# Mask transposition and mask-column copy one place later in a hand-ordered attention and feed-forward kernel

## The chip, the cores and the metric

The kernel runs on one core of one Trainium2 chip. The metric is the device time of one execution in microseconds. TensorE is called PE here (its weight loads PEld), VectorE DVE, ScalarE ACT, GpSimd POOL, and SyncE, which issues most transfers, SP.

## The reference

One transformer block in bf16 over 2048 tokens of width 640. The first half is linear attention with 32 heads of 20 features each: the feature map of queries and keys is a pair of softmaxes over a small per-head projection. The second half is a feed-forward layer of width 1728 with SiLU.

```python
qkv = x @ wqkv                                   # x is layernormed first
pq, pk = q @ w_phi, k @ w_phi                    # per head, 20 x 20
phi_q = concat(softmax(pq), softmax(-pq))        # 40 features per head
phi_k = concat(softmax(pk), softmax(-pk))
kv  = einsum("bhsf,bhsd->bhfd", phi_k, v)        # sum over all tokens
z   = einsum("bhsf->bhf", phi_k)
num = einsum("bhqf,bhfd->bhqd", phi_q, kv)
den = einsum("bhqf,bhf->bhq", phi_q, z) + 1e-6
h   = A_x + (num / den) @ wo
h2  = h + silu(layernorm(h) @ w1) @ w2
```

`kv` and `z` sum over all tokens, so no output of the attention can be formed before the last token's key features are there.

## The kernel before

**Tiling.** The 2048 tokens are 16 tiles of 128 (numbers 0 to 15), in four groups of four for the query side. Everything is held in SBUF; PSUM is one tile `mm` of eight banks of 512 f32.

**Order.** No scheduler decides the order. The string ORDER lists steps one after another, each a word such as `kn.7.d`: the function `op_kn` called with 7 and "d". Within each engine the instructions run in just the order in which the steps issue them; between engines they wait on semaphores where data demands it. A number behind @ names the PSUM banks. So a step's place in the list sets what it stands behind on every engine that it uses.

**Steps around the change.** For each key tile t:

- `kp.t`, `kq.t`: TensorE projects the normalised tokens by folded key weights (line 374); `ke.t`: ScalarE takes exp(+) and exp(-) into `Ek` (line 406).
- `kr.t`: VectorE sums each head's exponentials, `Sk` (a reduction of 1280 elements, line 414), and takes the reciprocal (line 417).
- `kn.t.how`: the key normalisation, `Ek` times the reciprocal. "p" gives all 64 head halves to POOL (1280 elements, line 425). "d" gives 16 of 64 to POOL (320 elements, line 425) and 48 to VectorE (960 elements, line 429); "b" halves it (640 each).
- `vp.t`, `vq.t`, `vc.t`: value projection and its copy out.
- `cc.t`: TensorE adds the K-V product of tile t into bank 7 of PSUM (32 small matmuls, line 438). It needs all of tile t's normalised `Ek`. The last of the sixteen is `cc.7`.

Then the sum is turned into the right operand of the query side, `KVBD`, a tile with, for each sign s, five row groups and three places of 22 columns each. `kc` copies the sum out by ScalarE (`KVT`, line 452) and transposes it in 32 x 32 blocks by VectorE (`KVF`, line 453); `km.0` and `km.1` multiply it by the mask `maskS` into columns 0 to 20 of each place (VectorE, line 456). Column 21 is the mask itself; it makes the denominator. The mask is made early by POOL as `maskR` (`mc`, lines 213 to 220). The step `mt` transposes `maskR` to `maskS` on VectorE (line 226, 480 elements) and copies one of its columns into column 21 of `KVBD` for both signs on POOL (line 230, two instructions of 15 elements).

`dp.t` (line 515) multiplies query features `EqT` by `KVBD`; `dw`, `dr`, `do` form the quotient (VectorE, and POOL at line 550), `td` transposes by a transfer, `op` applies `wo` (line 577), and the feed-forward half follows: `up` (line 656), `ua`, `yp` (line 702), `yh` (lines 666 and 715 take the odd 64 features).

Between the keys, the query projections `qp`, `qs`, `qr`, `qt` (line 468) with `qe` (ScalarE, line 490) are laid into TensorE's order as filling.

**The order before the change** around it: `... cc.8 kn.15.p cc.6 vp.7@4 vq.7 vc.7.a mt qp.0.2@6 cc.15 cc.14 kr.7 kn.7.d cc.7 qs.0.2 kc qp.3.0@0 qs.3.0 qr.3.0 close km.0 km.1 qe.0.2 dp.0@2 ...`. On VectorE `mt` thus stands ahead of tile 7's reduction, on POOL its two copies stand ahead of `kn.7.d`'s 320 elements.

Of the kernel before, what the change touches and what calls it, by code (L numbers as in the profile page):

```python
# [41 lines left out]
kn.5.b kq.14 kp.6@0 lo.0.2.s l2.8.10.s cc.5 kr.13 l1.3.s kn.4.p kn.10.p cc.3 cc.4 ke.14 kr.8 kn.8.p kr.14  # L42
cc.12 xd.7 cc.2 kq.6 ke.6 kr.6 kn.14.b kp.15@4 kq.15 ke.15 kr.15 qp.0.0@2 kp.7@0 kq.7 ke.7 kn.6.p qp.0.1@4
qs.0.1 qr.0.1 kn.13.d qt.0.1 qe.0.1 vp.14@0 vq.14 vc.14.a qs.0.0 qr.0.0 qt.0.0 qe.0.0 cc.10 cc.13 cc.8
kn.15.p cc.6 vp.7@4 vq.7 vc.7.a mt qp.0.2@6 cc.15 cc.14 kr.7 kn.7.d cc.7 qs.0.2 kc qp.3.0@0 qs.3.0 qr.3.0
close km.0 km.1 qe.0.2 dp.0@2 qt.3.0 qe.3.0 qp.2.0@6 qs.2.0 qr.2.0 qt.2.0 dw.0.p dr.0 dp.1@2 dw.1.p qp.1.0@0
qs.1.0 qr.1.0 do.0.0.p do.0.1.p dr.1 do.1.0.p qe.2.0 l2.0.2.s do.1.1.p qt.1.0 qe.1.0 qp.1.1@6 dp.3@2 qs.1.1
qr.1.1 td.0 td.1 dw.3.p dr.3 qt.1.1 do.3.1.p do.3.0.p qp.3.2@0 qp.1.2@1 dp.2@2 dw.2.p dr.2 do.2.1.p do.2.0.p
# [24 lines left out]
def kernel(  # L73
# [11 lines left out]
    nc = tc.nc  # L85

    P = nc.NUM_PARTITIONS
    T = 16
    D = 640
# [46 lines left out]
    wTk = first.tile([P, C, D], BF16, name="wTk")  # L136
# [116 lines left out]
        nc.sync.dma_start_transpose(wTq[:, :, c * P : (c + 1) * P], A_wqkv[c * P : (c + 1) * P, 0:D])  # L253

    def op_lt(c, q="s"):
        nc.sync.dma_start_transpose(wTk[:, :, c * P : (c + 1) * P], A_wqkv[c * P : (c + 1) * P, D : 2 * D])

    def op_lo(a, b, q="s"):
        dma(q, wo[:, a:b, :], A_wo[a * P : b * P].rearrange("(c p) n -> p c n", p=P))
# [509 lines left out]
```

## Time and profile before

| | |
|---|---|
| median of three runs | 236.86 us (236.83 to 236.92) |
| the profiled execution | 236.84 us |
| its span, first to last instruction | 235.0 us |
| PE busy | 230.1 us, 98% |
| DVE busy | 131.3 us, 56% |
| ACT busy | 114.2 us, 49% |
| POOL busy | 96.1 us, 41% |

The span is what the trace covers; the rest of the profiled execution's time lies around it. All places in the trace are microseconds from the span's start. A row of the timeline gives start, length, engine, line, operation, output<-input and shape, and in brackets the engine's idle time ahead of it with what ended it. Matmul ends are modelled and POOL's are rough. Neighbouring rows of one engine may overlap by some hundredths of a microsecond.

### The profile page before, as it was taken

The page shows a single profiled execution, that of the slowest core. Times are in us where ns is not written, and L with a number is a line of the kernel's source. Part 1 is how long each engine was busy: PE and PEld are TensorE (multiplying, and loading weights), DVE is VectorE, ACT ScalarE, POOL GpSimd, SP SyncE. Part 2 cuts the span into 40 slices and gives each one's busy share as a digit, 9 for nine tenths or more (in the row PEclk, how much of TensorE's full clock was granted, in tenths as well). Part 3 has the DMA queues.
Part 4 walks back from the last instruction along what each step waited for, and adds up shares of the span by engine and source line. Part 5 has one row for each costly group of instructions (what it writes and reads, how often), then busy time and mean ns, then how long its engine had stood idle before and what let it go on. Part 6 is the DMA issues. An engine that isn't in the chain of part 4 may idle for free.

```text
span 235.0 us, 6302 instructions
## 1 busy us (share of the span) xinstructions
PE 230.1 (98%) x2676; PEld 148.1 (63%) x2676; DVE 131.3 (56%) x250; ACT 114.2 (49%) x172; POOL 96.1 (41%) x188
## 2 busy tenths in 40 slices
PE   8999999999999999999999999999999999999995
PEld 3877777776644556876754654467666567567762
DVE  3999989979948899886985445030442001101132
ACT  3979798777748775843317152652010431330100
POOL 7477986997924462587166201326030000000000
PEclk9999999999999999999999999999999999999999
DMA  7977997970001585532815510211152010000012
GB/s 201 320 268 125 130 272 149 231 189 0 6 3 28 121 121 148 54 67 56 137 33 98 101 31 0 56 31 29 33 137 56 28 31 28 28 3 28 28 37 77
DMA packets 44844, 20.67 MB, mean 88 GB/s; under 512 B 34448, under 2 KB 44304, under 8 KB 44816
## 3 DMA queue, kind: packets, MB, share of 16 engines
q1 hardware_dynamic: 43728, 19.88, 38.4%
q10 hardware_dynamic: 1088, 0.39, 0.7%
q8 instruction: 21, 0.34, 0.6%
q14 instruction: 7, 0.06, 0.1%
HBM read 9.61 MB, written 2.62 MB: 52 GB/s over the span
## 4 chain that ended last, share of the span: by engine, by line
PE 70%; ACT 1%; DVE 0%; POOL 0%; issue 0%
PE mm L702 24%; PE mm L656 24%; PE mm L577 9%; PE mm L468 8%; PE mm L515 3%; PE mm L666 1%; PE mm L715 1%; ACT EqT L490 1%; DVE ob L732 0%; POOL Ek L425 0%; PE mm L438 0%
## 5 line engine op out<-in xcount | busy, mean ns | idle before, releaser
L702 PE MATMUL mm<-w,shT 128*128 128x320 bf16 (+2 forms) x416 | 59.0, 299 | 0.0
L656 PE MATMUL mm<-HnT,w 128*128 128x512 bf16 (+1 forms) x325 | 58.6, 337 | 0.0
L702 PEld LDWEIGHTS <-shT 128*128 128x128 bf16 x416 | 39.6, 98 | 17.7 <-issue 1.3
L678 ACT ACTIVATE shT<-mm 128x1024 bf16<-128x1024 f32 (+2 forms) x29 | 27.4, 962 | 47.6 <-PE mm L656 35.5
L656 PEld LDWEIGHTS <-w 128*128 128x128 bf16 x325 | 31.6, 98 | 23.6
L723 DVE TENSOR_TENSOR ob<-mm,X 128x640 bf16<-128x640 f32 x15 | 12.1, 818 | 60.0 <-PE mm L702 42.7
L374 PEld LDWEIGHTS <-XnT 128*128 128x128 bf16 x320 | 30.6, 98 | 12.0
L550 POOL TENSOR_TENSOR o<-u,rd 128x320 bf16<-128x320 f32 x25 | 18.7, 764 | 41.8 <-DVE rd L544 35.4
L425 POOL TENSOR_TENSOR Ek<-Ek,Sk 128x1280 bf16<-128x1280 bf16 (+2 forms) x16 | 33.6, 2118 | 4.5 <-DVE Sk L417 2.9
L594 ACT ACTIVATE sq<-X 128x640 bf16<-128x640 bf16 x16 | 11.7, 734 | 32.4 <-DVE X L586 29.5
L414 DVE TENSOR_REDUCE Sk<-Ek 128x64 f32<-128x1280 bf16 x16 | 23.3, 1455 | 2.6 <-ACT Ek L406 2.6
L374 PE MATMUL mm<-Wfk,XnT 128*128 128x320 bf16 x160 | 24.5, 299 | 0.0
L577 PE MATMUL mm<-wo,ot 128*128 128x320 bf16 x160 | 23.7, 300 | 0.3 <-ACT EqT L490 0.3
L468 PE MATMUL mm<-XnT,Wfq 128*128 128x512 bf16 x100 | 24.0, 380 | 0.0
L374 PE MATMUL mm<-wv,XnT 128*128 128x320 bf16 x160 | 23.5, 299 | 0.0
L490 ACT ACTIVATE EqT<-mm 128x1024 bf16<-128x1024 f32 (+1 forms) x24 | 19.7, 879 | 6.1 <-PE mm L468 6.0
L406 ACT ACTIVATE Ek<-mm 128x640 bf16<-128x640 f32 x32 | 20.6, 717 | 3.8 <-PE mm L374 1.8
L586 DVE SCALAR_TENSOR_TENSOR X<-mm,X 128x640 bf16<-128x640 f32 x16 | 12.9, 820 | 14.3 <-PE mm L577 14.0
L577 PEld LDWEIGHTS <-ot 128*128 128x128 bf16 x160 | 15.3, 98 | 6.9 <-issue 0.2
L468 PEld LDWEIGHTS <-Wfq 128*128 128x128 bf16 x100 | 9.1, 98 | 9.2
L536 DVE TENSOR_TENSOR u<-mm,w 128x672 f32<-128x672 f32 x16 | 13.7, 858 | 1.2 <-DVE w L534 0.2
L539 DVE TENSOR_TENSOR u<-u,mm 128x672 f32<-128x672 f32 x16 | 13.6, 853 | 0.6
(78 smaller groups left out, 204.9 us busy)
## 6 DMA issues: line engine op xcount, KB each, us to landing
out_dram<-ob SPq DMA_DIRECT2D x15, 160.0 KB, 1.8
w<-in_B_w_dram SPq DMA_DIRECT2D x6, 360.0 KB, 4.5
X<-in_A_x_dram SPq DMA_DIRECT2D x3, 640.0 KB, 6.6
w<-in_B_w_dram SPq DMA_DIRECT2D x5, 320.0 KB, 4.1
wk<-in_A_wqkv_dram SPq DMA_DIRECT2D x4, 160.0 KB, 4.2
wv<-in_A_wqkv_dram SPq DMA_DIRECT2D x1, 480.0 KB, 7.4
wo<-in_A_wo_dram SPq DMA_DIRECT2D x1, 480.0 KB, 5.9
w<-in_B_w_dram SPq DMA_DIRECT2D x1, 480.0 KB, 4.0
```

The costliest lines, as they stand in the source:

```text
L374: nc.tensor.matmul(ps[:, half, 0:320], tok(XnT[t // GT], t)[:, c, :], W[:, c, half * 320 : (half + 1) * 320], start=(c == 0), stop=(c == C ...
L406: nc.scalar.activation(Ek[:, s, :].rearrange("p (a n) -> p a n", a=2), tl["kp", t][:, :, 0:320], AF.Exp, scale=1.0 - 2.0 * s,)
L414: nc.vector.tensor_reduce(Sk[:], tl["ek", t][:].rearrange("p s (h f) -> p (s h) f", f=DH), axis=AX.X, op=ALU.add,)
L425: nc.gpsimd.tensor_tensor(Ek3[:, 0:n], Ek3[:, 0:n], Sk[:, 0:n].unsqueeze(2).to_broadcast([P, n, DH]), op=ALU.mult,)
L468: nc.tensor.matmul(tl["qp", g, i][:, k, :], Wfq[:, c, r * P : (r + 1) * P], XnT[g][:, c, :], start=(c == 0), stop=(c == C - 1),)
L490: nc.scalar.activation(E[:, s, rs[0] : rs[-1] + 1, :], tl["qp", g, i][:, 0 : len(rs), :], AF.Exp, scale=1.0 - 2.0 * s,)
L536: nc.vector.tensor_tensor(u[:], A[1][:, :, :, 0:21], w[:].unsqueeze(3).to_broadcast([P, 4, 8, 21]), op=ALU.mult,)
L550: (nc.vector if eng == "v" else nc.gpsimd).tensor_tensor(tl["o", t][:, a * 320 : (a + 1) * 320].rearrange("p (h f) -> p h f", f=DH), tl["u ...
L577: nc.tensor.matmul(ps[:, half, 0:320], tl["ot", t][:, c, :], wo[:, c, half * 320 : (half + 1) * 320], start=(c == 0), stop=(c == C - 1),)
L656: nc.tensor.matmul(ps[:, i * W : (i + 1) * W], w1[:, c, fc * P : (fc + 1) * P], HnT[g][:, c, 0:W], start=(c == 0), stop=(c == C - 1), skip ...
L678: nc.scalar.activation(sh[:, a:b], tl["up", g, k][:, 0 : b - a], AF.Silu)
L702: nc.tensor.matmul(ps, shT[g][:, fc * W + i * P : fc * W + (i + 1) * P], w2[:, fc, a:b], start=first and fc == 0, stop=last and fc == FC - ...
```

## The change

The word `mt` moves five words to the right in ORDER, from behind `vc.7.a` to behind `kn.7.d`. On VectorE that is past tile 7's reduction, reciprocal and multiplication; on POOL past tile 7's 320-element multiplication; the other words between issue nothing on these two engines. The second hunk lets the step `lt` choose a queue; no word `lt` stands in ORDER.

```diff
-kn.15.p cc.6 vp.7@4 vq.7 vc.7.a mt qp.0.2@6 cc.15 cc.14 kr.7 kn.7.d cc.7 qs.0.2 kc qp.3.0@0 qs.3.0 qr.3.0
+kn.15.p cc.6 vp.7@4 vq.7 vc.7.a qp.0.2@6 cc.15 cc.14 kr.7 kn.7.d mt cc.7 qs.0.2 kc qp.3.0@0 qs.3.0 qr.3.0
...
     def op_lt(c, q="s"):
-        nc.sync.dma_start_transpose(wTk[:, :, c * P : (c + 1) * P], A_wqkv[c * P : (c + 1) * P, D : 2 * D])
+        (nc.sync if q == "s" else nc.scalar).dma_start_transpose(wTk[:, :, c * P : (c + 1) * P], A_wqkv[c * P : (c + 1) * P, D : 2 * D])
```

## The prediction

> **What bounds the kernel now.** I read the first page of the profile first, then the chain of work that ended last in order of time, then the waits and the timeline of the stretch in which the change lies (58 to 74 us).
>
> ```profile
> span 235.0 us, 6302 instructions
> PE 230.1 (98%) x2676; PEld 148.1 (63%) x2676; DVE 131.3 (56%) x250; ACT 114.2 (49%) x172; POOL 96.1 (41%) x188
> PEclk9999999999999999999999999999999999999999
> ```
>
> TensorE (PE) is busy for 98% of the span at a full granted clock in every slice, so time can be won only where it stands still, and an engine off its path matters only where TensorE waits for it. The chain says where it did, from 65 us to the end:
>
> ```profile
> 65.26 0.65 POOL Ek L425
> 65.91 0.04 issue
> 65.95 0.37 PE mm L438 x32
> 66.33 2.27 PE mm L468 x10
> 68.59 0.40 PE mm L515 x38
> ...
> 86.91 0.02 issue
> 86.93 1.95 ACT EqT L490 x2
> 88.88 0.04 issue
> 88.92 1.52 PE mm L577 x10
> ...
> 232.29 0.29 DVE ob L732
> ```
>
> Columns are start, length, engine and line. The chain begins with one POOL instruction, the normalisation of token tile 7's keys (L425 in `kn.7.d`), on which TensorE's last K-V product (`cc.7`, L438) waits. After it the chain is TensorE's own work but for one stretch of ScalarE at 86.93, which itself followed matmuls. What starts `cc.7` earlier should thus move all that follows, to the end. How long TensorE stood there:
>
> ```profile
> PE mm L438 <- POOL Ek L425: 0.6, 1, 0.6
> ```
>
> ```profile
> 59.76 1.33 DVE L429 TENSOR_TENSOR Ek<-Ek,Sk 128x960 bf16<-128x960 bf16 x1
> 61.01 0.66 DVE L226 STREAM_TRANSPOSE maskS<-maskR 128x480 bf16<-128x480 bf16 x1
> 61.61 1.44 DVE L414 TENSOR_REDUCE Sk<-Ek 128x64 f32<-128x1280 bf16 x1
> 63.08 0.55 DVE L417 RECIPROCAL Sk<-Sk 128x64 f32<-128x64 f32 x1
> 63.74 1.27 DVE L429 TENSOR_TENSOR Ek<-Ek,Sk 128x960 bf16<-128x960 bf16 x1
> 63.94 1.32 POOL L230 COPY KVBD<-maskS 128x15 bf16<-128x15 bf16 x2
> 64.71 0.66 PE L438 MATMUL mm<-Ek,Vp 128*21 128x40 bf16 x64
> 65.18 0.72 POOL L425 TENSOR_TENSOR Ek<-Ek,Sk 128x320 bf16<-128x320 bf16 x1
> 65.95 0.37 PE L438 MATMUL mm<-Ek,Vp 128*21 128x40 bf16 x32 [0.58 <-POOL Ek L425]
> 66.44 0.42 ACT L452 CAST KVT<-mm 128x320 bf16<-128x320 f32 x1 [1.35 <-PE mm L438]
> 66.89 0.51 DVE L453 STREAM_TRANSPOSE KVF<-KVT 128x320 bf16<-128x320 bf16 x1 [1.89 <-ACT KVT L452]
> 67.44 0.57 DVE L456 TENSOR_TENSOR KVBD<-KVF,maskS 128x315 bf16<-128x315 bf16 x2
> 68.53 0.47 PE L515 MATMUL mm<-KVBD,EqT 32*128 32x44 bf16 x40
> 72.31 1.41 POOL L550 TENSOR_TENSOR o<-u,rd 128x320 bf16<-128x320 f32 x2 [6.41 <-PE mm L468]
> ```
>
> TensorE is through with `cc.15` and `cc.14` at 64.71 + 0.66 = 65.37 and starts `cc.7` at 65.95: 0.58 us of standing still. That is all there is to win here. Ahead of that wait lie, on POOL, the two mask copies (L230), and on VectorE (DVE) the mask transposition (L226). Both are moved behind tile 7's normalisation.
>
> **Part by part.** *VectorE.* The transposition leaves its place at 61.01, so tile 7's reduction starts 61.61 - 61.01 = 0.60 us earlier (its input is older: the reduction followed L226 without a wait), the reciprocal at 62.48, and the multiplication L429 is ready at 63.14 in place of 63.74. Whether that helps depends on POOL, whose single instructions in this stretch are:
>
> ```profile
> 57.36 2.71 POOL L425 TENSOR_TENSOR Ek<-Ek,Sk 128x1280 bf16<-128x1280 bf16 x1 [0.69 <-ACT Ek L406]
> ```
>
> ```profile
> 60.04 1.64 POOL L425 TENSOR_TENSOR Ek<-Ek,Sk 128x320 bf16<-128x320 bf16 x1
> ```
>
> ```profile
> 61.64 2.35 POOL L425 TENSOR_TENSOR Ek<-Ek,Sk 128x1280 bf16<-128x1280 bf16 x1
> ```
>
> ```profile
> 63.94 1.18 POOL L230 COPY KVBD<-maskS 128x15 bf16<-128x15 bf16 x1
> ```
>
> The same 320-element POOL instruction took 0.72 us at 65.18, with VectorE idle, and 1.64 us at 60.04, when L429 ran on VectorE until 59.76 + 1.33 = 61.09; it ended at 61.68, 0.59 us behind that. The first mask copy took 1.18 us (the second 0.25, below), and ended at 65.12, 0.11 us behind the other L429 (63.74 + 1.27 = 65.01). The other way round, both L429 of 960 elements ended exactly 1.02 us after the 1280-element POOL instruction in front of them: 61.09 against 57.36 + 2.71 = 60.07, and 65.01 against 61.64 + 2.35 = 63.99. So I read L429 on VectorE and the bf16 instructions on POOL as shutting each other out: who has begun, finishes, and the other waits.
>
> Then the 0.60 us on VectorE is worth nothing: L429, ready at 63.14, still waits for POOL's instruction of `kn.15` to end at 63.99, and ends at 63.99 + 1.02 = **65.01**, as before.
>
> *POOL.* With the copies gone from in front of it, the 320-element instruction of `kn.7` comes up at 63.94, finds VectorE waiting longer than itself, as at 60.04, and ends 0.59 us behind L429: 65.01 + 0.59 = **65.60**, against 65.18 + 0.72 = 65.90 before. Gain **0.30 us**. Its ends: if nothing of it were done during the wait, 65.01 + 0.72 = 65.73, gain 0.17; if the two engines did not shut each other out, all of TensorE's 0.58. I take 0.30, since the 60.04 row is the same instruction behind the same L429.
>
> The Trainium skill (SBUF — State Buffer, section "A bandwidth-pool intuition that's wrong (but worth ruling out)") says that a GpSimd operation behind a VectorE one on the shared port is blocked until the VectorE one ends plus about 115 ns. The copy's 0.11 us agrees. With a whole 0.72 behind it, the 320-element instruction would by that end at 65.01 + 0.115 + 0.72 = 65.85, an estimate from that page, and the gain would be 0.05; the 0.59 measured behind the earlier L429 speaks for the larger one.
>
> *TensorE* started `cc.7` 0.05 us behind POOL's end (65.90 to 65.95), so it starts at 65.65, and stands still for 0.28 us in place of 0.58.
>
> *The moved steps in their new place.* L226 (0.66) follows L429 at once and ends by 65.01 + 0.66 = 65.67. VectorE's next is L453, at 66.89 - 0.30 = 66.59 then: 0.9 us to spare. In its old place L226 ran its 0.66 beside a POOL instruction of the same kind, so I don't count it as shut out. The copies:
>
> ```profile
> L230 POOL COPY KVBD<-maskS x2: 247/713/1179, 63.9 to 65.0; 128x15 bf16<-128x15 bf16 x2
> ```
>
> Alone 0.25 us each, behind 65.67 they end at about 66.25. They are now due only where TensorE reads their column of `KVBD`, in `dp.0` (L515), which comes at 68.53 - 0.30 = 68.23: 2.0 us of cover, and VectorE's write of the same tile (L456, 67.14 then) comes 0.9 us behind them. POOL's next work is L550 at 72.31. So the move costs nothing as long as these two covers hold; without them every 0.1 us costs 0.1. Nothing is moved past a DMA; neither step issues one, and SP's order is unchanged. The changed `op_lt` is never called in ORDER: zero.
>
> *A wait more on TensorE.* In the built order L515's first weight load now waits for VectorE and its first matmul for POOL, once for each half of `KVBD`; before, only the matmul waited. Both semaphores are long up. Behind them stand all later matmuls. The nearest row is the one event instruction of that queue:
>
> ```profile
> L438 PEldq EVENT_SEMAPHORE  x1: 51/51/51, 65.2 to 65.2; - x1
> ```
>
> Between nothing and 2 x 0.05 = 0.10 us; it can't be less than nothing, since a wait starts nothing earlier. I take nothing: TensorE goes from L468 to L515 with loads ahead of matmuls, and a wait that is already met has only its issue to pay.
>
> **Sum.** The profiled execution took 236.84 us, 1.84 around its span of 235.0. 236.84 - 0.30 = 236.54; the median of the runs stands 0.02 above the profiled one, so **236.56 us**, 0.13% less. With the ends 0.17 and 0.41 (0.30 and the 0.11 by which the copy ended behind L429, if that handover were hidden too), and up to 0.10 for the waits, the forecast's own range is 236.45 to 236.75 (236.86 - 0.41, and 236.86 - 0.17 + 0.10 = 236.79, cut by a little).
>
> **The rivals.** *All of the stall goes.* If L429 can run at 63.14 beside POOL, it ends at 63.14 + 1.02 = 64.16 and POOL's 320 elements at 63.94 + 0.72 = 64.66, ahead of TensorE's 65.37. Then the 0.58 us go, and perhaps some of the overlap between one group of matmuls and the next: 64 matmuls took 0.66 and 32 took 0.37, so 32 add 0.29 and each group has 0.08 of run-out. 236.86 - 0.58 to - 0.66 gives 236.20 to 236.28. For it: the rows of POOL's instructions are only ends as recorded. Against it: twice the same 1.02 us from POOL's end to L429's, and two POOL instructions that end just behind L429's end. 0.20.
>
> *POOL goes first.* If POOL hands on from instruction to instruction, its 320 elements run at 63.94 to 64.66, and L429 from there to 65.68; `cc.7` starts at 65.73 and the gain is 0.22: 236.64, inside the forecast's range. Against it: at 60.04 and at 63.94 VectorE got in between. 0.07.
>
> *Slower: the mask column becomes the last input of `dp.0`.* The copies now share their moment with what VectorE does for `KVBD`. If they take the long row, 1.18 us each, from 65.67 to 68.03, the multiplication L456 (two inputs in SBUF like L429), ready at 67.14, is shut out until 68.03 and ends at 68.60; `dp.0` starts at 68.65 in place of 68.23, and 0.42 lost against 0.30 won makes 236.98. It decides from the moment that the copies end later than 68.23 - 0.05 - 0.57 = 67.61. Against it: the long row had L429 beside it, the short one didn't, and in the new place VectorE is idle but for L226. To lose over 0.2% the copies would have to end behind 68.38. 0.07.
>
> *Given back later* (a DMA or ScalarE result that TensorE meets 0.3 us sooner): 236.86. For it: the 86.93 row, where TensorE waits for ScalarE; against it: that one hangs on TensorE's own matmuls and moves with them. 0.06. *The change doesn't do what it says:* the built orders differ in just the moved rows. Nothing.
>
> **How the numbers follow.** Forecast 0.60, all of the stall 0.20, POOL first 0.07, given back 0.06, slower 0.07. The range reaches from the stall rival's lower end to the forecast's upper one, 236.2 to 236.75, and leaves about 0.13 out. 0.2% is 0.47 us, about what a measurement of this kernel can tell from no change; the forecast lies inside that. Below 236.39: the stall rival, 0.20, and a little of the forecast, 0.02. Above 237.33: 0.05 of the slower rival. Within: the rest, 0.73.
>
> **What would show it.** In the profile after: L429 of `kn.7` starting at 63.1 with a duration of about 1.87 us and ending near 65.0; POOL's 320-element instruction taking about 1.66 us from 63.94; TensorE's wait at L438 about 0.3 us; L226 at 65.0 and two short copies behind it; L515 at 68.2. L429 ending near 64.2 shows the stall rival; a copy over 1 us beside L456, or a wait of L515 on POOL, the slower one. A new wait of TensorE on a DMA would make the sum wrong.

## The result and the profile after

The changed kernel takes 236.45 us (median of 20 runs, 236.34 to 236.69) against 236.84 us of the kernel before (20 runs, 236.69 to 237.16): ratio 0.9984, 95% interval 0.9978 to 0.9991. That is 0.39 us less, with an interval of 0.21 to 0.52, against the 0.30 forecast. The change made the kernel a little faster, by less than the 0.2% that the prediction set as its bound.

The profiled execution took 236.37 us. From the first page of its profile:

```profile
span 234.7 us, 6283 instructions
PE 228.1 (97%) x2657; PEld 148.0 (63%) x2676; DVE 131.8 (56%) x250; ACT 114.2 (49%) x172; POOL 96.1 (41%) x188
```

PE counts 19 matmuls fewer only because their records are missing (PEld has all 2676). DVE is busy 0.5 us longer, though it runs the same instructions. Where that comes from is seen in the timeline of the stretch around the change (start, length, engine, line, operation):

```profile
59.70 1.33 DVE L429 TENSOR_TENSOR Ek<-Ek,Sk 128x960 bf16<-128x960 bf16 x1
60.95 1.47 DVE L414 TENSOR_REDUCE Sk<-Ek 128x64 f32<-128x1280 bf16 x1
62.46 0.55 DVE L417 RECIPROCAL Sk<-Sk 128x64 f32<-128x64 f32 x1
63.11 1.83 DVE L429 TENSOR_TENSOR Ek<-Ek,Sk 128x960 bf16<-128x960 bf16 x1
64.65 0.66 PE L438 MATMUL mm<-Ek,Vp 128*21 128x40 bf16 x64
64.86 0.67 DVE L226 STREAM_TRANSPOSE maskS<-maskR 128x480 bf16<-128x480 bf16 x1
65.58 0.37 PE L438 MATMUL mm<-Ek,Vp 128*21 128x40 bf16 x32 [0.27 <-POOL Ek L425]
65.60 0.40 POOL L230 COPY KVBD<-maskS 128x15 bf16<-128x15 bf16 x2
66.52 0.51 DVE L453 STREAM_TRANSPOSE KVF<-KVT 128x320 bf16<-128x320 bf16 x1 [0.98 <-ACT KVT L452]
68.15 0.47 PE L515 MATMUL mm<-KVBD,EqT 32*128 32x44 bf16 x40
71.94 1.41 POOL L550 TENSOR_TENSOR o<-u,rd 128x320 bf16<-128x320 f32 x2 [5.94 <-DVE rd L544]
```

And POOL's two instructions ahead of the copies, each from a narrow window of the same timeline:

```profile
61.58 2.35 POOL L425 TENSOR_TENSOR Ek<-Ek,Sk 128x1280 bf16<-128x1280 bf16 x1
```

```profile
63.89 1.64 POOL L425 TENSOR_TENSOR Ek<-Ek,Sk 128x320 bf16<-128x320 bf16 x1
```

Tile 7's multiplication on VectorE (L429) starts 0.63 us earlier than before (63.11 for 63.74) and lasts 0.56 us longer (1.83 for 1.27): nearly all that the departed transposition gave was spent waiting inside L429's own duration, until POOL's 1280 elements ended at 61.58 + 2.35 = 63.93. It ends at 64.94. POOL's 320 elements, up at 63.89, last 1.64 in place of 0.72 and end at 65.53, 0.59 behind L429. TensorE starts `cc.7` at 65.58, having stood still for 0.27 us in place of 0.58.

Since executions differ a little ahead of this stretch, I measure it from the start of the matmuls of `cc.15` and `cc.14` to the first product with `KVBD` (L515): before 68.53 - 64.71 = 3.82 us, now 68.15 - 64.65 = 3.50. That 0.32 us is the change's effect. The two profiled executions differ by more, by 236.84 - 236.37 = 0.47. Ahead of the stretch the changed kernel's trace is already 0.06 us earlier (64.65 for 64.71): its first load of X landed 0.09 us earlier, as the first VectorE row of each kernel shows, before and after:

```profile
3.89 0.49 DVE L274 BATCH_NORM_STATS2 stats<-X 128x6 f32<-128x320 bf16 x1 [3.89 <-DMA X<-in_A_x_dram]
```

```profile
3.80 0.49 DVE L274 BATCH_NORM_STATS2 stats<-X 128x6 f32<-128x320 bf16 x1 [3.80 <-DMA X<-in_A_x_dram]
```

From L515 on, the two traces run alike to the start of the last VectorE additions, before and after:

```profile
231.57 1.02 DVE L732 TENSOR_TENSOR ob<-mm,X 128x512 bf16<-128x512 f32 x2 [1.92 <-PE mm L702]
```

```profile
231.19 1.02 DVE L732 TENSOR_TENSOR ob<-mm,X 128x512 bf16<-128x512 f32 x2 [1.93 <-PE mm L702]
```

That is 231.57 - 68.53 = 163.04 before and 231.19 - 68.15 = 163.04 now: nothing was given back. The additions start 0.38 us earlier, which is 0.32 + 0.06; the other 0.09 of the 0.47 lies behind them and around the span, in time that the trace does not cover (1.84 us before, 1.67 now, from the rounded spans).

### The profile page after: what moved, and what is told of

It is laid out like the page before. It is cut to its first block, busy times and chain, and to the rows that moved or that the text cites. A ratio compares the mean times of both kernels' runs of the same rounds, so it can differ in the third digit from the quotient of the medians.

```text
span 234.7 us, 6283 instructions
## 1 busy us (share of the span) xinstructions
PE 228.1 (97%) x2657; PEld 148.0 (63%) x2676; DVE 131.8 (56%) x250; ACT 114.2 (49%) x172; POOL 96.1 (41%) x188
## 4 chain that ended last, share of the span: by engine, by line
PE 91%; POOL 2%; ACT 2%; DMA 1%; issue 1%; DVE 1%
PE mm L702 24%; PE mm L656 24%; PE mm L374 18%; PE mm L577 9%; PE mm L468 8%; PE mm L515 3%; POOL Ek L425 2%; PE mm L438 1%; DMA X<-in_A_x_dram 1%; PE mm L666 1%; PE mm L715 1%; PE mm L342 1%; ACT EqT L490 1%; ACT wTk L173 0%; PE mm L313 0%
## 5 line engine op out<-in xcount | busy, mean ns | idle before, releaser
L425 POOL TENSOR_TENSOR Ek<-Ek,Sk 128x1280 bf16<-128x1280 bf16 (+2 forms) x16 | 34.5, 2176 | 4.8 <-DVE Sk L417 3.7
L468 PE MATMUL mm<-XnT,Wfq 128*128 128x512 bf16 x90 | 22.1, 379 | 1.1 <-issue 1.0
```

The costliest lines, as they stand in the source:

```text
L425: nc.gpsimd.tensor_tensor(Ek3[:, 0:n], Ek3[:, 0:n], Sk[:, 0:n].unsqueeze(2).to_broadcast([P, n, DH]), op=ALU.mult,)
L468: nc.tensor.matmul(tl["qp", g, i][:, k, :], Wfq[:, c, r * P : (r + 1) * P], XnT[g][:, c, :], start=(c == 0), stop=(c == C - 1),)
```

## The experiments

**The theory:** VectorE's multiplication with two inputs in SBUF and POOL's bf16 instructions shut each other out, so on the path to `cc.7` lies the sum of POOL's `kn.15`, VectorE's `kn.7` and POOL's `kn.7`, plus whatever stands between them on POOL. Of the moved step only the two copies were part of that sum. **The first rival:** VectorE's 0.60 us earlier start brought the gain. **The second:** all instructions on tile 7's `Ek` are held in order for some other reason, with the memory of the inputs playing no part.

All medians and ratios below are against the kernel before on the same chip. "Stretch" is the one defined above, "wait" TensorE's at `cc.7`.

| kernel | stretch us | wait us | median us | before us | ratio (95% interval) |
|---|---|---|---|---|---|
| before | 3.82 | 0.58 | 236.84 | | |
| changed | 3.50 | 0.27 | 236.45 | 236.84 | 0.9984 (0.9978 to 0.9991) |
| changed_again | 3.51 | 0.28 | 236.55 | 236.96 | 0.9984 (0.9975 to 0.9992) |
| changed_third | 3.51 | 0.27 | 236.75 | 237.06 | 0.9985 (0.9976 to 0.9994) |
| copies_late | 3.50 | 0.27 | 236.62 | 236.97 | 0.9986 (0.9978 to 0.9995) |
| transpose_early | 3.81 | 0.59 | 236.98 | 236.97 | 1.0000 (0.9991 to 1.0009) |
| both_early | 3.50 | 0.27 | 236.72 | 236.97 | 0.9989 (0.9980 to 0.9998) |
| second_input_psum | 3.13 | none | 236.64 | 236.97 | 0.9984 (0.9975 to 0.9993) |
| second_input_psum_again | 3.14 | none | 236.63 | 236.96 | 0.9985 (0.9977 to 0.9994) |
| vector_all | 3.25 | none shown | 236.42 | 236.96 | 0.9981 (0.9972 to 0.9989) |
| vector_all_again | 3.26 | none shown | 236.39 | 237.06 | 0.9966 (0.9953 to 0.9979) |
| vector_all_psum | 3.12 | none | 236.26 | 237.06 | 0.9967 (0.9954 to 0.9979) |
| split_half | 3.71 | 0.48 | 236.93 | 236.96 | 1.0006 (0.9994 to 1.0018) |
| extra_idle | 3.51 | 0.27 | 236.90 | 237.06 | 0.9989 (0.9980 to 0.9998) |

A stretch is read from one trace; where the same kernel was traced again it came out within 0.01 us. A median here is of twenty runs in the first two rows and of eleven or twelve below (six and five for vector_all_psum and vector_all_again), and scatters by some 0.1 to 0.2 us. So the mechanism is read from the stretch and from the rows, the gain from the ratios.

### One half of the change alone

The step `mt` is cut in two: `mt` keeps the transposition, a new step `mu` makes the two copies.

```diff
 # copies_late, from the kernel before
+    def op_mu():
+        [nc.gpsimd.tensor_copy(KVBD[:, s, :, :, 21], maskS[:, :, :, 0]) for s in range(2)]
-kr.7 kn.7.d cc.7
+kr.7 kn.7.d mu cc.7
```

> Only the two mask copies move behind tile 7's key normalisation; the mask transposition stays ahead of tile 7's reduction, as in the kernel before. Theory (VectorE's two-input multiplication and POOL's bf16 instructions shut each other out, so only the copies were on the path): L429 of tile 7 is ready at 63.7, ends near 65.0, POOL's 320 elements end 0.59 behind it, TensorE waits about 0.28 us at the last K-V product, and the time is that of the changed kernel, 0.3 us (0.13%) under before. Rival (VectorE's 0.60 us earlier start brought the gain): the time is that of before, TensorE's wait 0.5 to 0.6 us.

```diff
 # transpose_early, from the kernel before, with op_mu
-ke.14 kr.8 kn.8.p kr.14
+ke.14 kr.8 mt kn.8.p kr.14
-vc.7.a mt qp.0.2@6
+vc.7.a mu qp.0.2@6
```

> The mask transposition moves into VectorE's idle stretch ahead of the reduction at 53.2 us; the two copies stay ahead of tile 7's 320 elements on POOL. So tile 7's reduction is 0.60 us earlier and the copies are still in the way. Theory: L429 of tile 7 starts at 63.1 but ends near 65.0 all the same, the first copy still takes over 1 us, TensorE's wait stays at 0.58 us and the time is that of before. Rival (VectorE's earlier start brought the gain): L429 ends near 64.2 to 64.4, TensorE's wait falls to 0.3 us or less, 0.3 us or more under before.

The two halves come out as far apart as they can. With only the copies moved, the stretch is the changed kernel's; the transposition still stands ahead of the reduction, and L429 starts as late as before, relative to its neighbours. The timeline of copies_late, and POOL's 320 elements from a narrow window:

```profile
61.11 0.67 DVE L226 STREAM_TRANSPOSE maskS<-maskR 128x480 bf16<-128x480 bf16 x1
63.83 1.27 DVE L429 TENSOR_TENSOR Ek<-Ek,Sk 128x960 bf16<-128x960 bf16 x1
65.64 0.40 POOL L230 COPY KVBD<-maskS 128x15 bf16<-128x15 bf16 x2
65.74 0.38 PE L438 MATMUL mm<-Ek,Vp 128*21 128x40 bf16 x32 [0.27 <-POOL Ek L425]
```

```profile
64.05 1.64 POOL L425 TENSOR_TENSOR Ek<-Ek,Sk 128x320 bf16<-128x320 bf16 x1
```

L429 ends at 63.83 + 1.27 = 65.10, and POOL's 320 elements end 0.59 us behind it, at 65.69, as in the changed kernel. With only the transposition out of the way, L429 starts early, lasts long, and nothing is won. The timeline of transpose_early:

```profile
61.21 1.47 DVE L414 TENSOR_REDUCE Sk<-Ek 128x64 f32<-128x1280 bf16 x1
63.37 1.83 DVE L429 TENSOR_TENSOR Ek<-Ek,Sk 128x960 bf16<-128x960 bf16 x1
64.14 1.32 POOL L230 COPY KVBD<-maskS 128x15 bf16<-128x15 bf16 x2
65.38 0.72 POOL L425 TENSOR_TENSOR Ek<-Ek,Sk 128x320 bf16<-128x320 bf16 x1
66.15 0.37 PE L438 MATMUL mm<-Ek,Vp 128*21 128x40 bf16 x32 [0.59 <-POOL Ek L425]
```

L429 ends at 63.37 + 1.83 = 65.20, the copies behind it, POOL's 320 elements at 66.10: the order of before, wait included. The first rival falls.

### The step's new place

```diff
 # both_early, from the kernel before, with op_mu
-ke.14 kr.8 kn.8.p kr.14
+ke.14 kr.8 mt kn.8.p kr.14
-ke.6 kr.6 kn.14.b
+ke.6 kr.6 mu kn.14.b
-vc.7.a mt qp.0.2@6
+vc.7.a qp.0.2@6
```

> The transposition in VectorE's idle stretch ahead of 53.2 us, and the copies in POOL's idle stretch at 54.7 us, both long before tile 7. Theory: as the changed kernel, TensorE's wait about 0.28 us, 0.3 us under before; where the step goes does not matter once the copies are away from tile 7. Rival (the new place behind tile 7's normalisation has a cost of its own, in the waits at the query product or in the copies beside VectorE's work on the same tile): up to 0.1 us faster than the changed kernel.

The stretch is again 3.50 us. In this kernel's order L515 waits for VectorE alone, as before the change. So neither the new wait of L515 on POOL nor the copies' nearness to L456 costs anything that the trace shows; the new place is free, and the earlier one, away from tile 7, does as well.

### What the shutting out hangs on

```diff
 # second_input_psum, from the changed kernel
-kr.7 kn.7.d mt
+ks.7@0 kt.7 mt
...
-        nc.vector.reciprocal(Sk[:], Sk[:])
+        tl["skp", t] = mm1()[:, 0:48]
+        nc.vector.reciprocal(tl["skp", t], Sk[:, 16:64])
+        nc.vector.reciprocal(Sk[:, 0:16], Sk[:, 0:16])
...
+            Ek3[:, 16:], Ek3[:, 16:], tl["skp", t].unsqueeze(2).to_broadcast([P, 48, DH]), op=ALU.mult,
```

The step `ks.7@0` puts 48 of the 64 reciprocals into PSUM bank 0, which is free then.

> The changed kernel, with tile 7's reciprocals of the 48 head halves that VectorE multiplies written to a free PSUM bank, so that L429's counterpart has one input in SBUF and one in PSUM; one small reciprocal more on VectorE for POOL's 16 halves. Theory (the shutting out comes from two SBUF inputs): VectorE's multiplication runs beside POOL's 1280 elements from about 63.2, for 1.0 to 1.1 us, ends near 64.3; POOL's 320 elements take 0.6 to 0.8 us from 63.9 and end near 64.6; TensorE does not wait at the last K-V product, and the time is 0.55 to 0.65 us under before. Rival (the two engines shut each other out for any reason bound to the shared tile Ek or to order): VectorE's multiplication ends near 65.0, and the time is that of the changed kernel.

The timeline, with L750 and L747 in the places of L429 and L425 of tile 7, and POOL's instruction ahead of them from a narrow window:

```profile
63.37 1.15 DVE L750 TENSOR_TENSOR Ek<-Ek,mm 128x960 bf16<-128x960 bf16 x1
64.23 0.72 POOL L747 TENSOR_TENSOR Ek<-Ek,Sk 128x320 bf16<-128x320 bf16 x1
64.97 0.94 PE L438 MATMUL mm<-Ek,Vp 128*21 128x40 bf16 x96
68.10 0.47 PE L515 MATMUL mm<-KVBD,EqT 32*128 32x44 bf16 x40
```

```profile
61.91 2.35 POOL L425 TENSOR_TENSOR Ek<-Ek,Sk 128x1280 bf16<-128x1280 bf16 x1
```

The same multiplication, writing the same tile at the same place, now runs from 63.37 to 64.52 straight through the last 0.89 us of POOL's 1280 elements (to 64.26), and POOL's 320 elements take 0.72 although 0.29 of that lies beside it. TensorE runs the 96 matmuls without a gap. What shut the two engines out was the second input in SBUF. The second rival falls. The Trainium skill (SBUF — State Buffer, section "Who interferes with whom") says that a VectorE instruction with two SBUF inputs contends with a GpSimd instruction that reads SBUF; the rows agree, 1.83 us with both inputs in SBUF and 1.15 with one in PSUM.

The median missed what was expected: 0.33 us under before, not 0.55 to 0.65. So it ran again beside the changed kernel.

> The changed kernel once more, beside the two that follow, so that differences of some 0.3 us between them can be told on one chip. Theory: the stretch from the start of the last three K-V products to the first query product is 3.50 us as in its first trace (3.82 before), and the time is 0.3 us under before. No rival is told apart by it.

> VectorE's second input in PSUM once more. Theory: the same stretch is 3.13 us, 0.37 us shorter than in the changed kernel, TensorE does not wait at the last K-V product, and the time is 0.6 to 0.7 us under before and 0.3 to 0.4 under the changed kernel of the same chip; what the first run of it lacked of that (it came out 0.33 us under before) was scatter of the first loads' landing. Rival (what the stretch wins is lost again later): the stretch is as short, but the time stands within 0.1 us of the changed kernel's, and the part behind the first query product is 0.3 us longer.

The stretch is 3.14 us, 0.37 shorter than the changed kernel's 3.51 on the same chip, and once more the median (236.63) stands 0.08 above the changed kernel's (236.55). The rival as I put it falls too: from L515 to the last addition this trace takes 231.27 - 68.14 = 163.13 us, the changed kernel's 231.49 - 68.46 = 163.03, a tenth and not three. The rest lies around the span. The span is on record for every execution, to 0.1 us: that of this kernel is 0.21 us shorter than the changed kernel's (means of eleven executions, 234.65 and 234.86), but 2.01 us lie outside it in place of 1.74, 0.27 more. So the 0.37 us are gone with that 0.27 and the 0.10 behind L515; the first statistics, at 4.17 us for 4.08, start a little later too.

### How the work is shared between the engines

```diff
 # vector_all, from the changed kernel
-kr.7 kn.7.d mt
+kr.7 kn.7.v mt
 # split_half, from the changed kernel
-kr.7 kn.7.d mt
+kr.7 kn.7.b mt
```

> The changed kernel with all of tile 7's normalisation on VectorE (1280 elements) and none on POOL. Theory (two-input work on VectorE and POOL's instructions shut each other out): VectorE's multiplication is ready at 63.1 but waits for POOL's 1280 elements to end at 63.9, ends 1.36 us behind that (1.02 x 1280/960), near 65.3; TensorE's wait is at most 0.1 us; 0.2 us or so under the changed kernel. Rival (they only slow each other where they work on the same tile, Ek of tile 7): VectorE's multiplication starts at 63.1 and lasts 1.36 us, ending near 64.5; TensorE's wait is nothing.

> The changed kernel with tile 7's normalisation halved, 640 elements on VectorE and 640 on POOL. Theory: VectorE's part ends 0.69 us behind POOL's 1280 elements, near 64.6, POOL's part 1.14 us behind that (1.27 less the 0.13 that it has done while waiting), near 65.8; TensorE waits about 0.5 us and the time is 0.2 us over the changed kernel, 0.1 under before. Rival (no shutting out): POOL's part runs from 63.9 for 1.27 us and ends near 65.2, ahead of TensorE's need; no wait, 0.3 us under the changed kernel.

The timeline of vector_all, then POOL's 1280 elements in it:

```profile
63.58 2.16 DVE L429 TENSOR_TENSOR Ek<-Ek,Sk 128x1280 bf16<-128x1280 bf16 x1
65.11 1.06 PE L438 MATMUL mm<-Ek,Vp 128*21 128x40 bf16 x96
```

```profile
62.04 2.35 POOL L425 TENSOR_TENSOR Ek<-Ek,Sk 128x1280 bf16<-128x1280 bf16 x1
```

L429 ends at 65.74, 1.35 us behind POOL's end at 64.39, where 1.36 was expected: POOL's `kn.15` has no part in tile 7, and still holds VectorE up. TensorE's 96 matmuls take 1.06 us in place of 0.94, so 0.12 of waiting is left, where at most 0.1 was expected. The stretch is 0.26 us under the changed kernel's, the median 0.13 (0.2 expected).

The timeline of split_half and POOL's rows:

```profile
63.28 1.50 DVE L429 TENSOR_TENSOR Ek<-Ek,Sk 128x640 bf16<-128x640 bf16 x1
65.96 0.38 PE L438 MATMUL mm<-Ek,Vp 128*21 128x40 bf16 x32 [0.48 <-POOL Ek L425]
```

```profile
61.75 2.35 POOL L425 TENSOR_TENSOR Ek<-Ek,Sk 128x1280 bf16<-128x1280 bf16 x1
```

```profile
64.06 1.85 POOL L425 TENSOR_TENSOR Ek<-Ek,Sk 128x640 bf16<-128x640 bf16 x1
```

POOL ends at 64.10, VectorE at 64.78 (0.68 behind, 0.69 expected), POOL's part at 65.91 (1.13 behind, 1.14 expected). The stretch is 3.71 us, 0.20 over the changed kernel's, as expected. The three shares put the sum's terms to the test at 0, 320 and 640 elements on POOL, and each end comes out within 0.02 us. The median was 0.38 us over the changed kernel's where 0.2 was expected; three of its twelve executions took 237.57 to 238.28 us, and what the median has beyond the stretch stays open.

### The start-up, and the best version

> The changed kernel beside the three that follow, as their base on one chip. Theory: 0.3 to 0.4 us under before, TensorE's wait at the last K-V product 0.27 us. It tells no rival apart by itself.

```diff
 # extra_idle, from the changed kernel
+    def op_xx():
+        nc.vector.reciprocal(ones4[:, 0:2], ones4[:, 0:2])
-ke.14 kr.8 kn.8.p
+ke.14 kr.8 xx kn.8.p
```

> The changed kernel and one small reciprocal more on VectorE (two elements of a tile that nothing reads), in its idle stretch ahead of 53 us. It asks where the 0.37 us went that the kernel with its second input in PSUM won in the stretch but not in its median. Theory (each program has its own start-up, the first load's landing and the time around the span, which moves by some tenths of a microsecond with the program): the stretch and the wait of 0.27 us are as in the changed kernel, and the median may stand up to 0.4 us off the changed kernel's, with the difference ahead of the first statistics or outside the span. Rival (start-up is the same for all): the median within 0.1 us of the changed kernel's.

The stretch is the changed kernel's; the median, 236.90, is 0.15 over its 236.75, between what the two expected, and the intervals of the two ratios overlap. The record of all executions tells where the 0.15 lies: the span is as long as the changed kernel's (means of 234.96 and 234.97 us), and outside it lie 1.95 us in place of 1.76. The other kernel with one VectorE instruction more, second_input_psum, has 1.96 and 2.01 there in its two sets. In all 33 executions of these two kernels it is 1.90 us or more; in no execution of the other kernels is it more than 1.89, and their means are 1.70 to 1.78. So both kernels with an instruction added on VectorE lost some 0.2 us outside the span, before any gain in the stretch could count; why is not shown.

```diff
 # vector_all_psum, from the changed kernel: tile 7 without POOL
-        nc.vector.reciprocal(Sk[:], Sk[:])
+        skp = mm1()[:, 0:64]
+        nc.vector.reciprocal(skp, Sk[:])
+        nc.vector.tensor_tensor(Ek3, Ek3, skp.unsqueeze(2).to_broadcast([P, 64, DH]), op=ALU.mult)
```

> All of tile 7's normalisation on VectorE, with the reciprocals in PSUM as its second input, none of it on POOL. Theory (two inputs in SBUF are what shuts the engines out): VectorE's 1280 elements run from 63.2 beside POOL's for about 1.5 us, end near 64.7, ahead of TensorE; no wait; the stretch is 3.13 us against 3.25 with all of it on VectorE from SBUF, 0.37 us under the changed kernel's, and unless start-up eats it the time is 0.6 to 0.7 us under before. Rival (VectorE waits for POOL whatever its second input): it ends near 65.7 as before, stretch 3.25 us.

> All of tile 7's normalisation on VectorE from SBUF, once more, on the chip of the others. Theory: VectorE's 1280 elements end 1.35 us behind POOL's, stretch 3.25 us, time 0.5 to 0.6 us under before. Rival (its first median, 0.54 us under before, was chance): the time is that of the changed kernel.

The timeline of vector_all_psum, then POOL's 1280 elements in it:

```profile
63.36 1.49 DVE L741 TENSOR_TENSOR Ek<-Ek,mm 128x1280 bf16<-128x1280 bf16 x1
64.87 0.93 PE L438 MATMUL mm<-Ek,Vp 128*21 128x40 bf16 x96
67.99 0.47 PE L515 MATMUL mm<-KVBD,EqT 32*128 32x44 bf16 x40
```

```profile
61.81 2.35 POOL L425 TENSOR_TENSOR Ek<-Ek,Sk 128x1280 bf16<-128x1280 bf16 x1
```

It runs as expected, 63.36 to 64.85, the first 0.80 us of it beside POOL's 1280 elements (to 64.16), and TensorE does not wait. This version, with no VectorE instruction more than the changed kernel, is the fastest in its median: 236.26 us against 236.75 for the changed kernel and 237.06 for the one before (ratio 0.9967, interval 0.9954 to 0.9979). All on VectorE from SBUF stands at 236.39 (0.9966, 0.9953 to 0.9979); the two can't be told apart by time, though their stretches differ by 0.14 us as the rows say. Both lie below the kernel before beyond their intervals; their intervals still overlap that of the changed kernel (0.9976 to 0.9994) by 0.0003, so a difference from it is likely but not shown.

## Why the prediction was right

- **What bounds the kernel.** Right: the stall of 0.58 us at `cc.7` was nearly all there was to win (without it, in second_input_psum, the stretch is 3.82 - 3.13 = 0.69 us shorter; the rest is the run-out between two groups of matmuls that the stall rival names), and what was won there reached the end whole (163.04 us from L515 on in both traces).
- **VectorE's 0.60 us.** Right that it is worth nothing: L429 was to be ready at 63.14 and end at 65.01; it started at 63.11 and ended at 64.94 (this trace is 0.06 us ahead of the other from before the stretch). transpose_early shows it alone: 0.01 us.
- **The copies' 0.30 us.** Right: POOL's 320 elements were to end at 65.60, and ended at 65.53, with the same 0.06 ahead. copies_late shows it alone: the stretch 0.32 shorter.
- **The choice of 0.59 behind L429's end,** not the whole 0.72, was right to 0.01 us. The estimate by the Trainium skill (SBUF — State Buffer, "A bandwidth-pool intuition that's wrong (but worth ruling out)") of 115 ns plus the whole instruction behind the release would have given a gain of 0.05. The page has the 115 ns from a transfer whose descriptors GpSimd writes, held up by a VectorE copy, not from a GpSimd tensor instruction. The 115 ns agrees with the small copy (0.11), but the 320-element instruction needed 0.13 less behind the release than alone.
- **The moved steps.** L226 was to start near 65.0 and the copies to be short: 64.86, and 0.40 for both, with L453 0.99 us behind L226's end and L515 2.15 behind the copies'. Both covers held.
- **The added wait at L515.** Right at nothing: both_early does without it and has the same stretch.
- **The rivals.** *All of the stall goes* fell; it takes another memory for one input, as second_input_psum shows. *POOL goes first* fell: VectorE, ready first, came in between POOL's 1280 elements and its next instruction in every trace read for it. *Slower* fell with the copies' 0.25 us each. *Given back later* fell with the 163.04 us.
- **The size.** 0.39 measured in the first 20 runs, 0.41 and 0.31 in the repeats, 0.30 forecast, 0.32 in the stretch. The forecast lies in every interval; the first median, 236.45 us, stands on the lower edge of the forecast's own range. The little that the first two medians show beyond the stretch is no term of the sum; it is of the size by which first loads and the time around the span differ.

## What to carry to other kernels

Where VectorE and POOL work on neighbouring pieces in SBUF, add them one behind the other as long as VectorE reads two inputs from SBUF, each with what it needs behind the other's end (here 1.02 us for 960 elements on VectorE and 0.59 for 320 on POOL); an earlier start of one then shows up as a longer duration, and even tiny POOL instructions in between cost time, here 0.30 us for two of 15 elements. Look for a duration that differs between equal instructions, and check whether equal remainders follow the other engine's end. A small second input put into PSUM frees both engines, and taking POOL off the last piece does nearly as well; an instruction added for it can cost more elsewhere than a gain of this size.

## What the runs showed of the hardware

- The waiting of either engine is counted in its busy time: L429 of 960 elements was 1.27, 1.33 and 1.83 us long in the traces before and after, and each ended 1.01 to 1.02 us behind POOL's end; POOL's 320 elements took 0.72 or 1.64.
- A VectorE multiplication of 960 elements with its broadcast input in PSUM took 1.15 us with POOL busy beside it, 1280 elements 1.49.
- The transposition on VectorE, with one input, took 0.62 us (both_early, at 51.77) to 0.67 (changed) beside POOL's instructions, and 0.67 with POOL idle (vector_all).
- The same program starts its first statistics between 3.80 and 4.08 us of its span from one execution to another, as the first load lands; with a gain of 0.3 us that is not small, and a stretch measured within the trace was the steadier scale.
- Two kernels with one VectorE instruction more than the others had 1.90 to 2.09 us of their time outside the span in each of 33 executions; all the others had 1.66 to 1.89.
